# Attention with a Fourier mixing and a channel block: in each stretch of filler work, the channel products ahead of the mixing's unit

## The chip, the cores and the metric

The kernel runs on one core of a Trainium2 chip. The metric is the device time of one execution in microseconds, as the median of several runs; for the kernel before it is 1695.95 us (three runs, 1695.81 to 1699.11). The profile shows one execution of 1697.3 us.

## The reference, cut to what matters

```python
# q, k, v: (8 batches, 8 heads, 576 positions, 64), fp32
scores = scale * q @ k.T
thresh = max(scores) - tau
attn   = exp(where(scores >= thresh, scores, -1e9) - max(scores))
attn   = attn / (sum(attn) + 1e-9)
x      = (attn @ v), heads side by side              # (8, 576, 512)

mixed = real(fft(fft(x, axis=1), axis=2))            # the mixing
u     = x + mixed
un    = (u - mean(u)) / sqrt(var(u) + 1e-6)
out   = u + relu(un @ w_ch1) @ w_ch2                 # the channel block, 512 -> 2048 -> 512
```

So there are three parts, one after the other for each batch: attention, the mixing, and the channel block. The batches are independent of each other, and this is what the kernel uses: while it does the attention of one batch, it does the mixing and the channel block of earlier ones.

## The kernel before: the parts concerned

Attention goes in steps. A step `i` is one tile of 128 query rows of a pair of heads (20 steps to a batch). The main loop, which handles batches 2 to 7 and one step more, issues the scores and the softmax of step `i`, and then the transposes of the weights of step `i - 1`; between these it calls `fill()` three times:

```python
    for i in range(2 * per_batch, total + 1):
        if i < total:
            scores(i)                     # TensorE: sc
            softmax(i)                    # VectorE: neg, den; ScalarE: e, thr
        ...
        prep = prep_in_parts(n + 1) if t == 3 and n + 1 < B * NPAIR else nothing
        weights = weights_in_parts(i - 1)
        next(prep, None)                  # (in one step of five) TensorE: pq
        fill()
        next(weights, None)               # TensorE: pe, pw; ScalarE copies: ends, e_t
        fill()
        next(weights, None)               # TensorE: pw; ScalarE copy: e_t
        next(prep, None)                  # pk
        fill()
        next(prep, None)                  # pt
        if t == 2:
            weighted_values(n, 0)         # TensorE: pv
        ...                               # (t == 0: weighted_values, folding of the rows)
        if i % per_batch == 0:
            start_batch(i // per_batch - 1)
    per_slot = cost(0) / 40
    while mixes or work:                  # the tail, with no attention left
        fill()
```

`fill()` is the function that the change concerns. It advances the mixing of a batch by one unit, if one is under way, and then the channel block until a budget is used up. The channel block of a batch may only begin when its mixing is complete (`work[0][0] < mixed`).

```python
    def fill():
        nonlocal budget, spent
        budget += per_slot
        if mixes:
            mix(1)
        while work and spent < budget and work[0][0] < mixed:
            done = next(work[0][1], None)
            if done is None:
                work.pop(0)
            else:
                spent += done

    def cost(g):
        n = tokens_of(g)[1]               # 256 tokens in a group, in all groups but two
        both = NJ * ND * n + NJ * DM * n // 128
        return 4 * (both if g < FIRST else both * 7 // 8) + ND * n     # 115,712 for 256 tokens

    def start_batch(b):
        nonlocal groups, todo, per_slot, budget
        mixes.append(mixing(b))
        todo += MIX                       # 19,240
        ...                               # groups of tokens are added to work
        keep = 0.4 * cost(0) + cost(1) if b == 0 else 4 * 7 * NK * DM // 2 * BT // 256
        per_slot = (todo - spent - keep) / (3 * per_batch)
        budget = spent
```

The mixing gives way (`yield`) after each of its units. The first three only fold the rows, on VectorE; the next eleven each hold a few matmuls of TensorE and a copy of their result out of PSUM, by ScalarE, or the use of it by VectorE:

```python
    def mixing(b):
        fold_chunks(nc.vector, b, 0);  yield 0                   # VectorE: f
        ...                                                      # VectorE: f (L673, L677)
        yield 0
        ...                                                      # VectorE: f (L673, L682)
        yield 0
        for u, r, n in ((0, 0, 128), (1, 128, 48), (2, 176, 128)):
            for odd in range(2):
                py = ps.tile([128, 512], FP32, tag="mm", bufs=4, name="py")
                ...                                              # TensorE: py <- f, L692
                nc.scalar.copy(y..., py...)                      # ScalarE: y_e or y_o, L697
                if not odd:
                    nc.scalar.copy(y[0:n, u, 256:257], py[0:n, 0:1])    # y_e, L702
                yield MIX / 11
        for t in range(2):
            pb = over_seq(y_o, 1, cols, 128)                     # TensorE: pa <- y_o
            nc.scalar.copy(sin, pb[:, 0:KH])                     # ScalarE: tmp, L724
            yield MIX / 11
            pa = over_seq(y_e, 0, cols, 128)                     # TensorE: pa <- y_e
            ...                                                  # VectorE: tmp (L728, L729),
            yield MIX / 11                                       # GpSimd: u_t (L731, L735)
            if t == 1:
                pa = over_seq(y_e, 0, slice(256, 257), 1)        # TensorE: pa <- y_e, one row
                nc.scalar.copy(sin[0:1, :], pa[0:1, 0:KH])       # L749
                ...
                yield MIX / 11
```

The channel block is done for groups of 256 tokens. Its second half is made of seven block products, each a sum of eight matmuls (L1090); after each pair of matmuls the generator gives way with 4 * DM = 2,048 units. A finished product is added to the rows on VectorE (L804); one accumulating sum keeps its PSUM buffer over several products, and some operands (`hs`, `s_tile`, L1086) are sums that GpSimd makes.

```python
        def product(bank, left, right, start):
            for p in range(NK):
                nc.tensor.matmul(bank[:, 0 : DM // 2], left[p], right[p], ...)
                if p % 2 == 1 and p < NK - 1:
                    yield 4 * DM
```

All of `pe`, `pw`, `pv`, `pq`, `pk`, `pt`, `py`, `pa`, `ph`, `po` and `pn` take their PSUM from one pool of four buffers (`tag="mm", bufs=4`); the scores have the other four banks. In the main loop the order of the instructions on TensorE is that of the program; on the other engines a scheduler decides it when the kernel is built.

Of the kernel before, what the change touches and what calls it, by code (L numbers as in the profile page):

```python
# [47 lines left out]
def kernel(  # L48
# [607 lines left out]
    MIX = 4 * (3 * 5 * 128 + 5 * 2 * KH)  # L656
# [506 lines left out]
    mixes = []  # L1163
    mixed = 0
    work = []
    spent = budget = per_slot = 0.0
    per_batch = NPAIR * NT

    def fill():
        nonlocal budget, spent  # L1170
        budget += per_slot
        if mixes:
            mix(1)
        while work and spent < budget and work[0][0] < mixed:
            done = next(work[0][1], None)
            if done is None:
                work.pop(0)
            else:
                spent += done

    total = B * per_batch
    groups = 0
# [123 lines left out]
    def mix(count):  # L1306
        nonlocal spent, mixed
        for _ in range(count):
            done = next(mixes[0], None)
            if done is None:  # L1310
                mixes.pop(0)
                mixed += 1
                break
            spent += done

    def second_batch(i):
# [29 lines left out]
        elif first == 2:  # L1346
            mix(2)
            transposed_weights(i - 1)
            mix(2)
            column_means(LAST)  # L1350
            copy_mean(LAST)
            mirrored(LAST)
            for c, eng in ((1, nc.vector), (3, nc.vector), (0, nc.gpsimd), (2, nc.gpsimd)):
                less_mean(eng, LAST, c)
            weighted_values(n, 0)
            advance(first)
            advance(first)
        else:
            fill()
            transposed_weights(i - 1)  # L1360
            advance(first)
            advance(first)
            fill()
            if t == 3:
                prep_pair(n + 1)
            fill()
            if t == 2:
                weighted_values(n, 0)
            if t == 0:
                weighted_values(n - 1, 1)  # L1370
                folds.append(fold_rows(n - 1))
                load_v(n + 1)
# [96 lines left out]
```

## Time and profile before

| | before |
|---|---|
| time, median of three runs | 1695.95 us |
| span of the profiled execution | 1697.3 us, granted TensorE clock 0.992 |
| TensorE busy | 1637.6 us |
| VectorE, ScalarE, GpSimd busy | 1137.2, 835.4, 585.6 us |
| HBM read, written | 46.02 MB, 9.44 MB (33 GB/s over the span) |

The page names PE for TensorE's matmuls, PEld for its weight loads, DVE for VectorE, ACT for ScalarE, POOL for GpSimd. The profile can be asked in several views: busy time by stretch of the span, with the clock that the throttle granted; groups of instructions by line; who waited for whom; and the timeline, in which neighbouring equal instructions are merged into one row. In a timeline row an fp32 matmul of the program counts as two records, so that a pair of products is a row of `x4`. A row that was waited for carries in brackets the idle time of its engine and what ended it; this tells which instruction was last to arrive, by the semaphores.

### The profile page before, as it was taken

How to read it: one execution, taken by the hardware profiler on the slowest of the kernel's cores; microseconds unless marked ns; L12 is line 12 of the kernel's file. 1: busy time of each engine (PE TensorE's matmuls, PEld its weight loads, DVE VectorE, ACT ScalarE, POOL GpSimd, SP SyncE). 2: the span in 40 equal slices, each digit the busy share in tenths (PEclk: the TensorE clock that was granted, in tenths of full speed). 3: DMA queues.
4: the chain of work that ended last, by engine and by line, in shares of the span. 5: the costliest groups of instructions: out<-in, count | busy, mean ns of one | idle time of the engine just before them, and what ended most of it. 6: DMA issues, size and time to landing. Idle time of an engine off the chain costs nothing.

```text
span 1697.3 us, 28896 instructions
## 1 busy us (share of the span) xinstructions
PE 1637.6 (96%) x10838; PEld 1280.9 (75%) x10838; DVE 1137.2 (67%) x2518; ACT 835.4 (49%) x1817; POOL 585.6 (35%) x779
## 2 busy tenths in 40 slices
PE   8998899999999999999999999999999999999998
PEld 4555555566887787878888778886878778789998
DVE  6885786556757576766566757676676758673454
ACT  5764675543545464645354546454646446442111
POOL 5773463040420442134332143223242144124332
PEclk9999999999999999999999999999999999999999
DMA  5323222010010101000101010100101000000000
GB/s 162 112 54 108 70 73 51 20 33 21 15 38 11 34 15 41 22 27 8 28 22 34 8 34 15 41 22 25 25 15 41 19 24 15 14 1 13 14 14 13
DMA packets 130384, 57.48 MB, mean 34 GB/s; under 512 B 121123, under 2 KB 121125, under 8 KB 130246
## 3 DMA queue, kind: packets, MB, share of 16 engines
q1 hardware_dynamic: 128854, 55.35, 12.1%
q8 instruction: 86, 1.41, 0.3%
q10 hardware_dynamic: 1392, 0.30, 0.1%
q14 instruction: 52, 0.43, 0.1%
HBM read 46.02 MB, written 9.44 MB: 33 GB/s over the span
## 4 chain that ended last, share of the span: by engine, by line
PE 75%; DVE 13%; ACT 8%; issue 2%; POOL 2%; DMA 0%; ACTq 0%; DVEq 0%; POOLq 0%
PE ph L926 23%; PE po L1090 18%; PE pv L589 9%; PE sc L433 7%; PE pw L560 5%; PE po L848 3%; ACT e L469 3%; DVE e L477 3%; DVE neg L461 3%; PE sc L444 2%; PE py L692 1%; PE ph L822 1%; DVE hs L1051 1%; DVE f L673 1%; PE pa L709 1%
## 5 line engine op out<-in xcount | busy, mean ns | idle before, releaser
L461 DVE TENSOR_REDUCE neg<-sc 128x1 f32<-128x576 f32 x288 | 205.7, 750 | 195.2 <-PE sc L433 183.3
L469 ACT ACTIVATE e<-sc,neg 128x576 f32<-128x576 f32 x288 | 212.0, 736 | 248.3 <-DVE neg L461 247.7
L477 DVE SCALAR_TENSOR_TENSOR e<-sc,thr,e 128x576 f32<-128x576 f32 x288 | 227.1, 813 | 59.6 <-ACT thr L473 58.8
L1090 PE MATMUL po<-w,hs 128*128 128x256 f32 x1024 | 248.6, 386 | 0.3 <-DVE u L804 0.3
L1090 PEld LDWEIGHTS po<-w,hs 128*128 128x128 f32 x1024 | 187.5, 192 | 33.3 <-issue 11.0
L926 PE MATMUL ph<-u_t,w 128*128 128x128 f32 x1536 | 187.5, 276 | 0.2 <-ACT u L788 0.2
L560 PE MATMUL pw<-ident,e 128*128 128x128 f32 x1152 | 170.9, 275 | 13.0 <-ACT ends L552 3.2
L926 PEld LDWEIGHTS ph<-u_t,w 128*128 128x128 f32 x1536 | 178.7, 192 | 4.9 <-issue 3.1
L433 PE MATMUL sc<-kT,qT 64*128 64x288 f32 x1024 | 167.0, 430 | 7.0 <-DVE e L477 6.4
L562 ACT COPY e_t<-pw 128x512 f32<-128x512 f32 x256 | 148.4, 593 | 47.3 <-PE pw L560 45.6
L935 DVE TENSOR_TENSOR hs<-ph,hs 128x512 f32<-128x512 f32 x160 | 107.3, 685 | 79.9 <-PE ph L926 56.6
L560 PEld LDWEIGHTS pw<-ident,e 128*128 128x128 f32 x1152 | 135.4, 141 | 32.2 <-issue 4.7
L433 PEld LDWEIGHTS sc<-kT,qT 64*128 64x128 f32 x1024 | 92.0, 186 | 68.4 <-issue 41.4
L926 PE MATMUL ph<-t_u,s_w 128*128 128x128 f32 x1024 | 126.1, 276 | 2.0 <-ACT ends L548 1.1
L804 DVE SCALAR_TENSOR_TENSOR u<-po,rstd,u 128x256 f32<-128x256 f32 (+1 forms) x164 | 76.2, 483 | 77.2 <-PE po L1090 75.4
L926 PEld LDWEIGHTS ph<-t_u,s_w 128*128 128x128 f32 x1024 | 119.3, 192 | 5.9 <-issue 2.3
L1090 PE MATMUL po<-hs,s_tile 128*128 128x256 f32 x512 | 122.0, 382 | 0.0
L943 ACT ACTIVATE hs<-hs 128x512 f32<-128x512 f32 x112 | 69.3, 629 | 70.9 <-DVE hs L935 70.8
L1090 PEld LDWEIGHTS po<-hs,s_tile 128*128 128x128 f32 x512 | 93.6, 190 | 13.6 <-issue 2.1
L496 ACT ACTIVATE e<-e,den 128x576 f32<-128x576 f32 x96 | 74.4, 775 | 53.2 <-DVE den L489 52.6
L1086 POOL TENSOR_TENSOR hs<-hs,s_tile 128x512 f32<-128x512 f32 x32 | 42.2, 1320 | 126.1 <-PE po L1090 120.1
L492 DVE TENSOR_SCALAR e<-e,den 128x576 f32<-128x576 f32 x120 | 81.4, 678 | 2.6
(199 smaller groups left out, 2886.0 us busy)
## 6 DMA issues: line engine op xcount, KB each, us to landing
hs<-in_moe_w_ch_dram SPq DMA_DIRECT2D x23, 512.0 KB, 4.3
out_dram<-u SPq DMA_DIRECT2D x36, 256.0 KB, 2.1
qk_in<-in_q_dram SPq DMA_DIRECT2D x64, 128.0 KB, 2.3
v_in<-in_v_dram SPq DMA_DIRECT2D x64, 128.0 KB, 2.3
qk_in<-in_k_dram SPq DMA_DIRECT2D x31, 128.0 KB, 2.4
w<-in_moe_w_ch_dram SPq DMA_DIRECT2D x6, 512.0 KB, 7.6
qk_in<-in_k_dram SPq DMA_DIRECT2D x31, 64.0 KB, 2.2
stage<-in_moe_w_ch_dram SPq DMA_DIRECT2D x3, 512.0 KB, 3.8
```

Source lines behind the costliest of these rows:

```text
L433: nc.tensor.matmul(sc[j][:, c, 0:HALF], qT[hp, 128 * t : 128 * t + 128], kT[hp, HALF * c : HALF * (c + 1)], start=True, stop=True,)
L461: nc.vector.tensor_reduce(out=neg[:, j : j + 1], in_=sc[j][:, :, 0:HALF], axis=AXIS_XY, op=ALU.max, negate=True,)
L469: nc.scalar.activation(out=ej, in_=sc[j][:, :, 0:HALF], func=ACT.Exp, bias=neg[:, j : j + 1], scale=1.0)
L477: nc.vector.scalar_tensor_tensor(out=ej, in0=sc[j][:, :, 0:HALF], scalar=thr[:, j : j + 1], in1=ej, op0=ALU.is_ge, op1=ALU.mult, accum_out ...
L492: nc.vector.tensor_scalar(out=e[:, 0:S], in0=e[:, 0:S], scalar1=den[:, 0:1], scalar2=None, op0=ALU.mult)
L560: nc.tensor.transpose(pw[:, c, :], e[:, c0 : c0 + 128], ident[:, :])
L562: nc.scalar.copy(e_t[:, 4 * j : 4 * j + 4, qs], pw[:, :, :])
L589: nc.tensor.matmul(pv[64 * j : 64 * j + 64, 0:m], vt[:, 2 * c + j, :], e_t[:, 4 * j + c, 0:m] if c < 4 else ends[:, 0:m], start=(c == 0), ...
L804: nc.vector.scalar_tensor_tensor(out=u, in0=product, scalar=self.rstd[:, t : t + 1], in1=u, op0=ALU.mult, op1=ALU.add,)
L926: nc.tensor.matmul(banks[name][:, 128 * q : 128 * q + 128], left[c][:, 512 * part + 128 * q : 512 * part + 128 * q + 128], right[c], start ...
L935: nc.vector.tensor_tensor(out=to, in0=bank, in1=to if other is None else other, op=ALU.add)
L1090: nc.tensor.matmul(bank[:, 0 : DM // 2], left[p], right[p], start=start and p == 0, stop=p == NK - 1, skip_group_check=True,)
```

## The change

In `fill()` the two parts change places: the channel block's products come first, and the mixing's unit last. So that the sum of a stretch keeps to the budget, the products stop one unit's worth (`MIX / 11`) earlier while a mixing is under way. Nothing is added or taken away of the computation.

```diff
     def fill():
         nonlocal budget, spent
         budget += per_slot
-        if mixes:
-            mix(1)
-        while work and spent < budget and work[0][0] < mixed:
+
+
+        reserve = MIX / 11 if mixes else 0
+        while work and spent + reserve < budget and work[0][0] < mixed:
             done = next(work[0][1], None)
             if done is None:
                 work.pop(0)
             else:
                 spent += done
+        if mixes:
+            mix(1)
```

It is for what the unit's first matmul needs: the folded rows `f` from VectorE, the copies of the units before it, and a free PSUM buffer have some more time to arrive while TensorE works on products. A second effect follows from the code: when the mixing of a batch ends in a stretch, the channel block of that batch may begin only in the next one.

## The prediction

> **What bounds the kernel.** I read the page first (engine shares, slices), then TensorE's waits, then the timeline of the stretches in which a batch is mixed.
>
> ```profile
> PE 1637.6 (96%) x10838; PEld 1280.9 (75%) x10838; DVE 1137.2 (67%) x2518; ACT 835.4 (49%) x1817; POOL 585.6 (35%) x779
> ...
> PE   8998899999999999999999999999999999999998
> ```
>
> TensorE is busy 96% of the span, and in the slices it falls below nine tenths only in the first two batches and the last slice. The change moves matmuls and adds none, so it can only change the gaps between them. The largest groups of them around the mixing, by the waits of TensorE:
>
> ```profile
> PE py L692 <- ACT ends L548: 5.3, 4, 1.5
> PE pw L560 <- ACT ends L552: 3.2, 4, 1.3
> PE pa L709 <- ACT e_t L564: 2.7, 4, 0.7
> ...
> PE pw L560 <- ACT y_e L702: 2.2, 1, 2.2
> ```
>
> Columns are total us, times, longest. Around the mixing, a matmul wants a PSUM buffer or an operand that ScalarE has not yet copied out. The timeline gives the places. Mixing stretches that use the changed function begin near 318, 533, 723, 955, 1144, 1331 and 1514 us. Their gaps sum to 1.15, 4.20, 1.46, 3.59, 3.59, 3.60 and 2.13 = **19.7 us**. In three of them the clock also falls (slices of 4 us and of 25 us):
>
> ```profile
> 536.00:540.00 4.00, 2.78 (x10) 2.51 (x11) 4.00 (x13) 2.70 (x8) 0.00 (x0) 0.63 0.01 2
> ...
> 950.00:975.00 25.00, 22.84 (x136) 16.82 (x135) 19.99 (x45) 11.96 (x28) 5.54 (x4) 0.93 0.01 2
> ```
>
> The third number from the end is the granted clock: 0.63 over 4 us loses 1.5 us, 0.93 over 25 us loses 1.75. Three dips cost about 5.2 us. So 19.7 + 5.2 = 25 us, 1.5%, is all that better order could give: faster by 2% is out of reach.
>
> This is the first step of the stretch at 1144, TensorE, then ScalarE, then VectorE, and last one row of its end (start, us, line, tile; in brackets the idle time before and what ended it):
>
> ```profile
> 1142.66 1.24 PE L433 MATMUL sc<-kT,qT 64*128 64x288 f32 x8
> 1143.83 0.66 PE L692 MATMUL py<-dim_c,f 128*128 128x65 f32 x4
> 1144.82 0.49 PE L692 MATMUL py<-dim_c,f 128*128 128x128 f32 x2 [0.33 <-DVE f L673]
> ...
> 1148.69 0.71 PE L692 MATMUL py<-dim_s,f 128*128 128x128 f32 x4 [1.49 <-ACT ends L548]
> ...
> 1145.35 0.63 ACT L697 COPY y_e<-py 128x256 f32<-128x256 f32 x1 [2.57 <-PE py L692]
> ...
> 1147.74 0.74 ACT L469 ACTIVATE e<-sc,neg 128x576 f32<-128x576 f32 x1 [1.77 <-DVE neg L461]
> 1148.38 0.26 ACT L548 COPY ends<-pe 128x128 f32<-128x128 f32 x1
> ...
> 1146.90 1.41 DVE L461 TENSOR_REDUCE neg<-sc 128x1 f32<-128x576 f32 x2
> ...
> 1177.51 0.41 PE L709 MATMUL pa<-seq_even,y_e 128*1 128x145 f32 x2 [0.68 <-ACT e_t L564]
> ```
>
> What to see: the scores are ready at 1143.8, but VectorE takes their maximum only at 1146.9, because the folds of the mixing stand ahead in its queue. ScalarE's first exponential follows at 1147.7. Now y_e is copied *before* that exponential, while ScalarE is otherwise idle; only the later copy of ends is caught behind it.
>
> **What the Trainium skill says.** *PSUM — Partial Sum Buffer*, "Engine vs sequencer instructions": ScalarE's queue is strictly first in, first out. The trace agrees: ends, whose matmul ran before 1146.6, is copied at 1148.38, after an exponential. *Perfetto Trace Analysis*, "Matmuls": independent groups should rotate through PSUM banks so that a copy overlaps the next group. Here only four buffers serve everything but the scores, and the 2.18 us wait at 537 is such a rotation falling short. *TensorE: Matmul & The Clock Gate*, "Part 1: The HAM clock gate": half rate after a mostly idle free-running window of about 3.4 us, for about as long. The trace fits in part: a gap of 2.18 us cost 1.5 us of clock; gaps of 1.49 us did so at 960 and 1335, but not at 1148 (1.00 in that slice).
>
> **The change part by part.** A stretch (a call of fill) has a budget, on average 4,660 units: (2.25 groups x 115,712 + 19,240) / 60 by the kernel's own formulas. A mixing unit counts 1,749, a pair of products 2,048. Before, the unit is issued first; after, products run until only 1,749 is left, then the unit. No instruction is added. But each unit comes one pair later in TensorE's total order, and stands directly ahead of the transposes pe and pw instead of a pair ahead. A pair (a row of x4 at L1090) takes 0.87 us (1149.24 to 1150.11, the next row).
>
> The compiled order shows what the scheduler makes of this:
>
> 1. *First unit, stretches at 955, 1144, 1331.* ScalarE now has both exponentials, then y_e, then ends. The buffers are worse too: one holds the sum, one a finished product not yet added, one a product in progress; py, pe and pw all take the fourth in turn. So pe waits for y_e, and pw for ends. Working it at 1144: scores one pair earlier, ending 1143.0; two pairs 1.75, then py, last part released by the fold at 1144.8: py ends 1145.45. The fold at L682 ends at 1145.6; after it VectorE has one instruction of 0.68 ahead of the maximum instead of three, so the maximum starts at 1146.25. ScalarE, by the rows before: 0.84 from there to the first exponential (1146.90 to 1147.74), 0.64 + 0.19 + 0.62 for it, thr and the second, 0.63 for the two y_e copies: pe at about 1149.1, ends, pw at 1149.7. From there pw, two pairs, py, pw, py48 take 0.43 + 1.75 + 0.45 + 0.43 + 0.53: pv (the weighted values, which start at 1152.28 in the timeline before) at 1153.3. **+1.1 us each**. TensorE now stands 4.1 us nearly unbroken instead of 2.1, so I expect a clock dip in all three stretches, against two before: +1.7 once.
> 2. *Second step.* The copy of the fourth unit moves from between to behind the exponentials, and pw needs its buffer. By the same durations pw starts 3.05 us after the scores instead of 2.42. **+0.6** at 533, 723, 955, 1144 and 1331, **+3.1** in all.
> 3. *End of the mixing.* A pair now stands ahead of the last unit, where 0.68 us was idle (1177.51), and ahead of a unit that idled 0.21. **-0.9** at 955, 1144 and 1331, -0.7 at 533: -3.3.
> 4. *Stretch at 318.* py waited 1.15 us for y_e; a 1.72 us pair now covers it: **-1.15**.
> 5. *At 533.* The wait for y_e stays about 2 us with its dip: -0.2.
> 6. *At 723.* y_e also falls behind the exponentials; pw then waits 1.65 where py waited 0.85: +0.6, less the 0.61 us wait for t_u near 767, since the next group starts after pv and the scores; an extra dip at even chances: +0.8 together.
> 7. *Tail at 1514.* No softmax. The 1.20 us wait goes, but the last unit has one pair less behind it to cover GpSimd's additions: the wait of 0.93 grows by as much as 0.9: -0.3.
>
> Sum: 3.3 + 1.7 + 3.1 - 3.3 - 1.15 - 0.2 + 0.8 - 0.3 = **+4.0 us**, so 1695.95 + 4.0 = 1700.0.
>
> **Rivals.** *A. The order pays.* The unit's input folds get 0.87 us more, and products fill TensorE where it idled. For it: every gap named in 3, 4 and 7. If the copies behind the exponentials cost nothing, items 1, 2 and 6 vanish and some 5 to 10 us are won: 1686 to 1691. Against it: VectorE, not TensorE, is late in the first step, and the compiled ScalarE order puts y_e behind the exponentials. *B. PSUM becomes the bound.* If the shared buffer and the clock hit harder, with two half-rate windows per stretch and knock-on waits of GpSimd's sums, five stretches lose 3 us more each: about 1712. Against it: stalls let the other engines catch up. *C. Hidden anyway*: gains and losses cancel, 1696; the per-item sizes here are all near 1 us, so this is close to my own case.
>
> **Range and chances.** Items have an uncertainty of 0.5 to 1 us in each of seven stretches, partly shared, plus the dips: about 6 us either way, more on the lower side because A removes known gaps. 1691 to 1707. Two per cent is 34 us; the gain is capped at 25, and a loss that size would need 5 us in every stretch: 0.01, 0.97, 0.02.
>
> **What would show it.** Right: in the first steps near 955, 1144 and 1331, pe or pw waits some 3 to 4 us for y_e and ends, and the clock dips in each; near 1156, pw waits about 0.7 us for y_o; the 0.68 us wait for e_t and the 1.15 us one at 323 are gone. The sum of busy time stays. Wrong: y_e copied before the exponentials; no wait at pe; or an added wait of products for GpSimd's sums, which I take to be hidden.

## The result, and the profile after

The changed kernel takes 1701.65 us (median; 1699.14 to 1703.76), the kernel before 1696.68 us in the same comparison. The ratio is 1.0026, with a 95% interval of 1.0007 to 1.0046: slower by some 4.4 us by the ratio (the medians differ by 5.0), well within 2%. The prediction was 1700.0.

The page of the changed kernel (busy time and share of the span):

```profile
PE 1636.9 (96%) x10838; PEld 1290.8 (76%) x10838; DVE 1133.7 (67%) x2518; ACT 836.0 (49%) x1817; POOL 583.6 (34%) x779
```

As many matmuls as before, TensorE as busy as before: the page alone tells nothing. TensorE's waits do (us in total, times, longest):

```profile
PE pe L541 <- ACT y_e L702: 8.1, 3, 2.8
...
PE pw L560 <- ACT y_e L702: 4.7, 2, 2.6
PE pw L560 <- ACT y_o L697: 3.0, 6, 0.6
...
PE ph L926 <- POOL u_t L731: 2.3, 1, 2.3
```

Gone are the waits of `py` for `ends` (5.3 us, four times) and of `pa` for `e_t` (2.7 us, four times). New are three waits of `pe` for `y_e`, a second one of `pw` for `y_e`, and waits for `y_o`; one for `u_t` has grown from 0.9 us.

The first step of the stretch at 1144, from the timeline (start, us, engine, line, tile; in brackets the idle time before, and what ended it), TensorE, ScalarE, VectorE:

```profile
1142.59 1.24 PE L433 MATMUL sc<-kT,qT 64*128 64x288 f32 x8
1143.76 1.13 PE L1090 MATMUL po<-hs,s_tile 128*128 128x256 f32 x4
1144.72 1.03 PE L1090 MATMUL po<-w,hs 128*128 128x256 f32 x4
1145.59 0.83 PE L692 MATMUL py<-dim_c,f 128*128 128x65 f32 x6
1149.11 0.33 PE L541 MATMUL pe<-ident,e 128*128 128x128 f32 x1 [2.69 <-ACT y_e L702]
1149.80 0.84 PE L560 MATMUL pw<-ident,e 128*128 128x128 f32 x4 [0.36 <-ACT ends L548]
1150.43 1.91 PE L1090 MATMUL po<-w,hs 128*128 128x256 f32 x4
...
1146.99 0.74 ACT L469 ACTIVATE e<-sc,neg 128x576 f32<-128x576 f32 x1 [3.90 <-DVE neg L461]
...
1147.82 0.73 ACT L469 ACTIVATE e<-sc,neg 128x576 f32<-128x576 f32 x1
1148.44 0.61 ACT L697 COPY y_e<-py 128x256 f32<-128x256 f32 x1
...
1146.15 1.41 DVE L461 TENSOR_REDUCE neg<-sc 128x1 f32<-128x576 f32 x2
```

`py` is finished at 1146.4, but ScalarE copies it out only at 1148.44, behind both exponentials, which waited for VectorE's maximum. The pair of products behind the wait takes 1.91 us in its row, where a row of the same kind takes 1.03 at 1144.72: TensorE runs at half rate. The clock (third number from the end) over slices of 4 us, here and in the same step of the stretch at 955:

```profile
1148.00:1152.00 4.00, 2.53 (x9) 2.06 (x10) 4.00 (x12) 2.58 (x6) 0.00 (x0) 0.77 0.00 0
...
960.00:964.00 4.00, 3.64 (x13) 3.05 (x13) 2.98 (x10) 1.53 (x3) 0.43 (x1) 0.50 0.00 0
964.00:968.00 4.00, 4.00 (x29) 3.36 (x29) 0.00 (x0) 1.94 (x4) 0.85 (x1) 0.77 0.00 0
```

In the stretches concerned, the profile of before has three such dips (536, 960, 1336) and that of after six (536, 728, 960, 1150, 1338, 1548). By the clock records of the traces a dip lasts 3.41 us; the one at 960 in the profile of after lasts twice as long. So there are three such windows at half rate before and seven after.

### The profile page after: what moved, and what is told of

It is laid out like the page before. It is cut to its first block, busy times and chain, and to the rows that moved or that the text cites. A ratio compares the mean times of both kernels' runs of the same rounds, so it can differ in the third digit from the quotient of the medians.

```text
span 1701.4 us, 28902 instructions
## 1 busy us (share of the span) xinstructions
PE 1636.9 (96%) x10838; PEld 1290.8 (76%) x10838; DVE 1133.7 (67%) x2518; ACT 836.0 (49%) x1817; POOL 583.6 (34%) x779
## 4 chain that ended last, share of the span: by engine, by line
PE 77%; DVE 12%; ACT 8%; issue 2%; POOL 1%; DVEq 0%; ACTq 0%
PE ph L926 23%; PE po L1090 19%; PE pv L589 9%; PE sc L433 7%; PE pw L560 6%; PE po L848 3%; ACT e L469 3%; DVE neg L461 3%; DVE e L477 3%; PE sc L444 2%; DVE hs L1051 1%; PE py L692 1%; PE ph L822 1%; PE pd L112 1%; PE pa L709 1%
## 5 line engine op out<-in xcount | busy, mean ns | idle before, releaser
L804 DVE SCALAR_TENSOR_TENSOR u<-po,rstd,u 128x256 f32<-128x256 f32 (+1 forms) x164 | 76.3, 483 | 72.1 <-PE po L1090 70.9
L731 POOL TENSOR_TENSOR u_t<-x,tmp 128x289 f32<-128x289 f32 (+1 forms) x47 | 35.0, 751 | 142.9 <-DVE tmp L728 125.0
```

Source lines behind the costliest of these rows:

```text
L804: nc.vector.scalar_tensor_tensor(out=u, in0=product, scalar=self.rstd[:, t : t + 1], in1=u, op0=ALU.mult, op1=ALU.add,)
```

## The experiments

The ratios are to the kernel before, run next to each on the same chip (its medians are 1696.2 to 1697.6 us). A profile shows one execution, whose time can lie a few us off the median.

| Kernel | us | ratio (95% interval) |
|---|---|---|
| changed kernel | 1701.65 | 1.0026 (1.0007 to 1.0046) |
| late units alone in the new order | 1693.08 | 0.9975 (0.9965 to 0.9985) |
| new order, tail in the old | 1699.28 | 1.0012 (1.0003 to 1.0020) |
| old order with the reserve | 1688.75 | 0.9944 (0.9931 to 0.9956) |
| new order, softmax later | 1690.03 | 0.9952 (0.9939 to 0.9966) |
| new order, waits filled with repeats | 1697.66 | 0.9998 (0.9990 to 1.0006) |
| new order without the reserve | 1704.26 | 1.0038 (1.0025 to 1.0050) |
| old order, reserve, late units new | 1687.86 | 0.9944 (0.9932 to 0.9956) |
| old order, reserve, softmax later | **1683.26** | **0.9914 (0.9900 to 0.9929)** |
| old order, softmax later | 1684.66 | 0.9937 (0.9924 to 0.9951) |
| the same with twice the reserve | 1686.46 | 0.9940 (0.9928 to 0.9953) |
| reserve, softmax later, late units new | 1685.67 | 0.9937 (0.9924 to 0.9949) |

The theory: the order costs by ScalarE's copies that fall behind the exponentials, and gains at the end of the mixing. The rivals: that TensorE's clock dips carry the difference, and that the pair held back (the reserve), not the order, is what costs.

### Is the gain at the end of the mixing real?

The new order is kept for the last five units of a mixing alone, and not in the tail. (Against the kernel before. `units` counts the units of a mixing that are done, folds included; `tail` is empty until attention ends. Their bookkeeping is left out.)

```diff
+        last = units >= 9 and not tail
-        if mixes:
+        if mixes and not last:
             mix(1)
-        while work and spent < budget and work[0][0] < mixed:
+        reserve = MIX / 11 if mixes and last else 0
+        while work and spent + reserve < budget and work[0][0] < mixed:
...
+        if mixes and last:
+            mix(1)
```

> New order (products first, unit last, one pair held back) only for the five units that end a mixing while attention goes on; old order for the folds, the six py units and the whole tail. My theory (the loss comes from y_e and y_o copied behind the exponentials in the first two steps of a stretch, the gain from a pair of products ahead of the last units): the first two steps look as before the change (a wait for ends of about 1.5 us and no wait of pe for y_e at 955, 1144, 1331), the waits of 0.68 and 0.21 us at the end of the mixing are gone: 1692 to 1693.5 against about 1696.5 before, that is 3 to 4 us faster. The rival that clock dips at random, not the waits, make the difference: anything from 1695 to 1702. The rival that holding back one pair costs by itself wherever it is done: no gain, 1696 to 1698.

1693.08 us, about 4 us faster than the kernel before, as the theory has it. In its trace the waits of `pa` for `e_t` are gone, and the waits of the first steps are those of before. Between the same scores on either side of the stretch at 1331, where its trace and that of before both have a dip, it wins 0.95 us.

### Is the tail a cost of its own?

The tail alone goes back to the old order. (Against the changed kernel.)

```diff
-        reserve = MIX / 11 if mixes else 0
+        last = not tail
+        if mixes and not last:
+            mix(1)
+        reserve = MIX / 11 if mixes and last else 0
...
-        if mixes:
+        if mixes and last:
             mix(1)
```

> The new order everywhere except in the tail after the last softmax, which has the old order. My theory of the tail (the last unit has fewer products behind it to cover GpSimd's additions, so the wait for u_t grew from 0.93 to 2.33 us and brought a clock dip): the wait returns to about 0.9 us, no dip near 1546, and the time is 2 to 2.5 us below the changed kernel, about 1699. If the tail's loss came from work arriving late from earlier stretches: no change, about 1701.5.

1699.28 us, 2.4 below the changed kernel. The two intervals overlap, so the medians alone don't settle it; but between the last scores and the end the profile takes 2.4 us less than that of the changed kernel, the same as that of before. A row of GpSimd of the changed kernel, then two of TensorE, show why the tail costs:

```profile
1544.33 0.68 POOL L731 TENSOR_TENSOR u_t<-x,tmp 1x289 f32<-1x289 f32 x1
...
1540.74 1.99 PE L1090 MATMUL po<-hs 128*128 128x256 f32 x8
1545.07 2.89 PE L926 MATMUL ph<-u_t,s_w 128*128 128x128 f32 x16 [2.33 <-POOL u_t L731]
```

Two pairs (x8) stand behind the last unit, where before four did (x16). GpSimd needs till 1545.0 all the same. With the old order in the tail the wait is as before, and the dip at 1548 is gone:

```profile
PE ph L926 <- POOL u_t L731: 0.9, 1, 0.9
```

### Order or reserve?

```diff
-        while work and spent < budget and work[0][0] < mixed:
+        reserve = MIX / 11 if mixes else 0
+        while work and spent + reserve < budget and work[0][0] < mixed:
```

> The old order (unit first in each stretch), but products stop one unit's worth (about one pair) earlier in each. It does the shift of the budget alone. My theory (the order decides, since with the unit first y_e is copied ahead of the exponentials): within 1 us of before, about 1696 to 1697.5, and no wait of pe for y_e at 955, 1144, 1331. The rival (the pair held back makes the loss): as the changed kernel, about 1701.

Both expectations were wrong: 1688.75 us, 8.4 *below* the kernel before. The missing corner of the table of two by two is the new order without the reserve:

```diff
-        reserve = MIX / 11 if mixes else 0
+        reserve = 0
```

> The changed kernel without the reserve: products run until the budget of the stretch is spent, then the unit. With the kernel before, the changed one and the run with the old order and the reserve this fills the table of two by two. If the reserve's gain of 8.4 us, seen with the old order, is independent of the order: 1708 to 1711. If the reserve helps only where a unit stands first: as the changed kernel, 1700 to 1703.

1704.26 us, between the two expectations. In its trace `pw` waits for `y_e` up to 4.2 us (15.3 us, four times). So the change consists of two parts of opposite sign, which don't simply add:

| us against the kernel before | no reserve | reserve | what the reserve does |
|---|---|---|---|
| unit first | 0 | -8.4 | -8.4 |
| unit last | +6.6 | +5.0 | -1.6 |
| what the order does | +6.6 | +13.4 | |

(Each is a median less that of the kernel before beside it. The -1.6 lies within the noise of its two runs; that the reserve does less with the unit last, -1.6 against -8.4, does not. An edit of TensorE's order also changes the order that the scheduler gives the other engines, so a cell stands for the whole kernel that results.)

The first step at 1144 with the old order and the reserve (this run is 6.8 us ahead there), TensorE, then VectorE:

```profile
1138.35 0.49 PE L692 MATMUL py<-dim_c,f 128*128 128x128 f32 x2 [0.55 <-DVE f L673]
...
1139.54 0.27 PE L541 MATMUL pe<-ident,e 128*128 128x128 f32 x1
...
1141.44 0.71 PE L692 MATMUL py<-dim_s,f 128*128 128x128 f32 x4 [1.19 <-ACT ends L548]
...
1137.38 0.47 DVE L804 SCALAR_TENSOR_TENSOR u<-po,rstd,u 128x256 f32<-128x256 f32 x1
1137.78 0.96 DVE L673 SCALAR_TENSOR_TENSOR f<-f,factors 128x304 f32<-128x304 f32 x2
1138.67 0.46 DVE L682 TENSOR_TENSOR f<-sums 128x304 f32<-128x304 f32 x1
...
1139.65 1.41 DVE L461 TENSOR_REDUCE neg<-sc 128x1 f32<-128x576 f32 x2
1140.99 0.86 DVE L804 SCALAR_TENSOR_TENSOR u<-po,rstd,u 128x256 f32<-128x256 f32 x2
```

In the kernel before, two additions of L804 (0.86 us together) stood between the last fold and the maximum, and `pe` waited 0.26 us for one of them. With the reserve both come behind the maximum (at 1140.99), and one earlier addition stands ahead of the folds. The maximum starts 2.58 us after the scores' end instead of 3.07. The waits of this step sum to 1.74 us instead of 2.08. After the first two batches TensorE's gaps sum to 22.5 us instead of 25.6, and no window there, up to the last 40 us of the run, is at half rate, where before has three, which lost 5.1 us of clock (some 4 us of time at the price found below). These two make 7 to 8 us. This is a reading of two traces: that the reserve is worth 8.4 us is measured, but no run tests by itself that the place of the additions is what makes it so.

### Do the waits cost, or the clock?

More work, put into the wait: the first unit's matmuls write the same values into the same buffer three times more, in the mixings near 955, 1144 and 1331.

```diff
-                for c, c0, c1 in SIN if odd else COS:
+                again = 3 if 4 <= b <= 6 and u == 0 and not odd else 0
+                for c, c0, c1 in (SIN if odd else COS) + again * (SIN if odd else COS):
```

> The changed kernel, in which the matmuls of a mixing's first unit are issued three times more into the same PSUM buffer, in the mixings near 955, 1144 and 1331. They write the same values again, so nothing is computed that wasn't; 1.33 us of the 2.7 us wait for y_e that follows is then filled with work. ScalarE copies y_e only behind the exponentials, so the copy should not come later. If the clock's dips carry the loss in these three stretches (the rows suggest 1.6 us and more each): no slices under 0.98 there, and 3 to 6 us below the changed kernel, 1696 to 1698.5. If the waits themselves carry it: no change, 1701 to 1702.

1697.66 us: 54 matmul records more (10892), and 4 us less than the changed kernel; it is level with the kernel before. The repeats fill 2.0 us of the wait (the row of `py` takes 2.84 us instead of 0.83), not 1.33. (Lines behind the edit are one higher in this kernel.) The timeline of TensorE:

```profile
1142.36 2.84 PE L693 MATMUL py<-dim_c,f 128*128 128x65 f32 x24
1145.90 0.33 PE L541 MATMUL pe<-ident,e 128*128 128x128 f32 x1 [0.71 <-ACT y_e L703]
...
1147.29 1.03 PE L1091 MATMUL po<-w,hs 128*128 128x256 f32 x4
```

The clock over 1148 to 1152 us:

```profile
1148.00:1152.00 4.00, 4.00 (x36) 3.42 (x36) 1.09 (x3) 2.54 (x6) 1.76 (x1) 1.00 0.02 4
```

`pe` starts 6.54 us after the start of the scores (1139.36), in the changed kernel 6.52: the wait for `y_e` ends just as late. But the pair behind it takes 1.03 us in its row instead of 1.91, and the next scores start at 1152.73, 13.37 us after the first, instead of 14.81 (1157.40 - 1142.59). So **1.44 us of this stretch is the clock's answer to the idle time in the wait.** Over whole stretches, from scores to the same scores, the changed kernel takes 2.45, 1.42 and 1.26 us more than the one with repeats at 955 (two windows at half rate), 1144 and 1331: some 1.3 us for a window. Without the dip this stretch takes 0.09 us less than before (same scores on either side; before has no dip here either). In the three late stretches the new order's longer waits and its gains cancel, and what remains is dips.

### Can the copies be put ahead of the exponentials?

```diff
-            softmax(i)
+            if not mixes:
+                softmax(i)
...
         next(prep, None)
+        held = i < total and mixes
         fill()
+        if held:
+            softmax(i)
```

> The new order, with the softmax of a group issued after the first stretch of products and units when a mixing is under way, so that ScalarE copies y_e and ends ahead of the exponentials. My theory: the waits of pe for y_e of 2.7 us at 955, 1144 and 1331 vanish, but VectorE then takes the maximum some 2 us later, and the wait moves to the second step, where a unit waits for y_o behind the exponentials by about 2 us: within 2 us of the changed kernel, 1699 to 1703. If the copies' place in ScalarE's queue were all there is to it: 4 us or more below the changed kernel, 1697 or less.

1690.03 us, 11.6 below the changed kernel: the second case of the expectation. ScalarE now copies `y_e`, `ends` and one `e_t` ahead of the exponentials. The waits of `pe` are 1.6 us (for `u` from VectorE), the wait of 0.5 us for `y_o` is gone in the three late stretches, and none of these has a dip; the stall in the second step that I expected did not come. With the old order, without and with the reserve:

> The kernel before, with only the softmax issued after the first stretch of a step while a mixing is under way; old order, no reserve. With the reserve this move won 5.5 us. If the two are independent: about 1691 to 1692.5. If the softmax's place matters only because the reserve has made the first step short: 1695 to 1698.

> The old order with the reserve, and the softmax issued after the first stretch of a step while a mixing is under way, so that y_e and ends are copied ahead of the exponentials. If the wait of 1.19 us for ends is then gone without a new one: about 1 us less in each of five stretches, 1683 to 1686. If the later maximum moves the wait to the second step: 1688 to 1692.

1684.66 us, below both expectations, and 1683.26 us. Each is compared with the kernel before that ran beside it: the move is worth 11.6 us without the reserve and about 6 with it (14.4 less 8.4). So the two overlap, and without the reserve it does more than I took from the run with it: my 5.5 was only what the reserve had left over. What the reserve adds on top, some 3 us, is at the edge of what the intervals tell apart. In the trace without the reserve one dip is left, at 536. ScalarE's rows in the step at 1144, without the reserve and then with it:

```profile
1138.43 0.27 ACT L548 COPY ends<-pe 128x128 f32<-128x128 f32 x1 [1.37 <-PE pe L541]
...
1141.12 0.74 ACT L469 ACTIVATE e<-sc,neg 128x576 f32<-128x576 f32 x1 [0.98 <-DVE neg L461]
```

```profile
1136.14 0.74 ACT L469 ACTIVATE e<-sc,neg 128x576 f32<-128x576 f32 x1 [1.40 <-DVE neg L461]
1136.78 0.26 ACT L548 COPY ends<-pe 128x128 f32<-128x128 f32 x1
```

Without the reserve the move does what it is for: `ends` is copied ahead of the exponential, and the wait of 1.49 us for it is gone in the three late stretches. In its place `pe` waits 0.8 to 0.9 us for `u`, and `pv` 0.80 us for `e_t`. With the reserve `ends` still stands behind the first exponential, as it did without the move, and `py` waits 1.6 us for it in each of the late three. So 1683.26 us lies in the range of the first case, but not by its reason: that case took the wait for `ends` to be gone. What went is the rest: the waits for `f`, and at the end of the mixing those of `pw` and `pa`. The gaps of this fastest kernel after the first two batches sum to 17.8 us against 25.6, and no dip is left there. Gaps 7.8 and dips 4 to 5 make some 12 to 13 of the 14 us.

### Attempts to go further

In the first, one line differs from the fastest kernel; the other two join parts that were run before:

```diff
-        reserve = MIX / 11 if mixes else 0
+        reserve = 2 * MIX / 11 if mixes else 0
```

> As the fastest so far (old order, reserve, later softmax), but with twice the reserve, so that two pairs are held back until the mixing ends. My theory (one pair held back helps because the scores and the unit come earlier than VectorE's queue fills; a second brings TensorE to the folds before they are done): the waits for f and for ends in the first step grow by up to 0.87 us in each of five stretches: 1684 to 1688. If the reserve helps by its length: 1676 to 1680.

> The old order with the reserve, but the new order from the tenth unit on while attention goes on. If the 0.95 us that the late units gained in each of three stretches (and some at 533 and 723) comes on top of the reserve's gain: 1684.5 to 1686.5. If the reserve had gained the same waits already: 1688 to 1689.5.

> As the fastest so far (old order, reserve, later softmax), with the new order from the tenth unit on while attention goes on. The waits at the end of the mixing that the late new order took away (0.68 and 0.21 us) are no longer in the trace of the fastest, so it should bring nothing: 1682.5 to 1684.5. If the late new order gains by itself: 1680 to 1682.

1686.46, 1687.86 and 1685.67 us. Twice the reserve loses 3 to 4 us against once: the first unit waits 0.89 us for `f` in the late three stretches, and `py` 2.05 us at 318, so one pair was the right amount of these two. The late new order, worth 4 us by itself, brings nothing that can be told from the reserve alone (both 0.9944), and nothing on top of both, where it is slower if anything (0.9937 against 0.9914, intervals that overlap); there its time lies above both expectations. None of the three beats the fastest.

## Why the prediction was right, and where it was not

The starts of the same scores in both profiles give what each stretch added. (Both profiles are of executions some 2 us above the median of their kernel. Both sums leave out 1.5 us by which the profile of after was ahead before the first stretch; the change does not touch that part.)

| Stretch | 318 | 533 | 723 | 955 | 1144 | 1331 | tail | sum |
|---|---|---|---|---|---|---|---|---|
| predicted | -1.2 | -0.3 | +1.4 | +0.8 | +2.5 | +0.8 | -0.3 | +4 |
| measured | -0.1 | -1.3 | +2.9 | +0.9 | +1.3 | -0.4 | +2.4 | +5.7 |

The total was right, and so was the mechanism of the late stretches: `y_e` behind the exponentials, a wait of `pe` for it, and a dip in each. But single terms were off by up to 2.7 us and made up for each other, so that 1700.0 came this close to 1701.65 is in part luck.

1. *First unit.* `y_e` is copied behind both exponentials, and `pe` and `pw` wait for `y_e` and `ends`, 2.7 and 0.36 us, in all three stretches. The size of +1.1 was too large: I had `pe` 6.1 us after the scores' end, the trace has 5.35 (1149.11 - 1143.76), because I held VectorE's folds in place while the scores came a pair earlier, and the folds came earlier with them. Without the dip, the start of `pv` moves by +0.43 us (1150.27 with the repeats, 1152.28 before, less the 2.44 by which that run was ahead); with it by +1.86 (1154.93 - 1152.28 - 0.79).
2. *Second step.* `pw` waits 0.49 us for `y_o`. Predicted +0.6, measured +0.34 (the step's start to the next scores' start).
3. *End of the mixing.* -0.9 predicted, -1.0 measured in the run with repeats (between the scores at 1163.7 and at 1184.2 of before and the same ones there); -0.95 in the run with only the late units changed.
4. *318.* The wait of 1.15 us for `y_e` is gone, as predicted. But 1.02 us of wait for `ends` stands at 310.6 where 0.36 was; I had not foreseen a new wait there. What remains of the difference to -1.15 I can't name.
5. *533.* The wait for `y_e` stayed (2.05 us), with its dip. It came out better by 1 us than the sum of its three items; at the end of the mixing the 0.68 us for `e_t` went, and 1.34 us for `ends` fell to 0.85.
6. *723.* `pw` waits 2.65 us, not 1.65, and the dip that had even chances came.
7. *Tail.* **Here the sign was wrong**, -0.3 predicted and +2.4 measured. I let the growth of the wait for `u_t` and the loss of the wait of 1.20 cancel, with one pair less behind the last unit. It is two pairs less; the wait grew by 1.4 us, not 0.9, TensorE fell to half rate behind it, and of the 1.20 there remained 0.56. The run with the old tail gives back 2.4 us.

The dips were the largest term that was mis-sized. I had one and a half more than before, at 1.7 us, so 2.6 us; the profile of after has four half-rate windows more. At 1.3 us each they make some 5 of the 5.7 us (an estimate; the windows at 723 and in the tail were not isolated), and leave less than 1 for all waits and gains together, where the prediction without its dips had 1.5. So the loss is mostly the clock's, and what sets the clock off is the waits that the order made.

The rivals: *A* (copies behind exponentials cost nothing) is contradicted by the waits for `y_e`. But its number, 1686 to 1691, was reached with the copies moved ahead. *B* was right in kind, since the clock hits harder than I had it, but not in size (1712). What no item had is that the change consists of two parts: I worked out the pair held back only as a shift of the unit, and missed that alone it is worth -8.4 us. The ceiling of 25 us held: the best kernel found wins 14.

## What to carry to other kernels

Where an engine is 96% busy, a new order of its queue is worth what it does to the *other* engines' queues: look up which copy falls behind which long instruction, and move that instruction before moving the matmuls. Take a change that does two things apart before judging it; here one half by itself won 8 us, and the other on top of it lost 13. And price a wait of TensorE with the half rate that can follow (some 1.3 us here): if the wait can't be removed, even repeated matmuls in it can pay, as they won 4 us here.

## What the runs showed that was not expected

*TensorE: Matmul & The Clock Gate*, "Part 1: The HAM clock gate", of the Trainium skill speaks of an idle window of about 3.4 us that runs free of the kernel. That it has to be only mostly idle was the prediction's own reading, not the page's. The runs bear out both, and put a number to "mostly". The traces hold the times at which the clock was lowered. In each of the thirteen profiles these times lie whole multiples of 3.413 us apart (to 0.01 us), as on a grid, and from 300 us to 40 us ahead of the end a dip fills one or two windows of this grid. There are 5140 such windows in all. In 27 of them TensorE is idle for 1.745 us or more, 51% of the window, and behind 26 of these the next window is at half rate. Of the other 5113 only three are followed by one, and two of those three are themselves at half rate. (The limit is read off these same windows.)

So the idle time within one window of the grid decides, and not the length of a gap. This answers what the prediction left open: why the gap of 1.49 us brought a dip at 960 but not at 1148. Here is the kernel before, cut on its grid (length, TensorE busy, ..., clock third from the end):

```profile
956.87:960.28 3.41, 1.66 (x10) 0.99 (x9) 3.41 (x7) 1.64 (x6) 0.00 (x0) 1.00 0.00 0
960.28:963.69 3.41, 3.41 (x12) 2.69 (x12) 3.38 (x11) 1.65 (x4) 0.56 (x1) 0.50 0.00 0
1144.60:1148.01 3.41, 2.12 (x11) 1.43 (x11) 3.41 (x8) 0.90 (x3) 0.00 (x0) 1.00 0.00 0
```

At 960 the gap shares its window with one of 0.27 us, 1.75 us idle together. At 1148 a border of the grid at 1148.01 divides it, and the window ahead of the border has 1.29 us. The grid lies differently against the kernel in each profile (its first border anywhere between 0.5 and 3.3 us), so a wait of 1.5 to 2 us is a risk of a dip and not a certainty, and executions of one kernel differ: of 48 of the kernel before, the 31 with a mean clock of 0.994 have a median of 1697.1 us, and the 8 with 0.992 one of 1699.2 us.
